# The last 64 channels of gate and up: one pair of half-height products, or two full ones with zero rows in the weight tiles

## The chip, the cores and the metric

The kernel runs on one core of one Trainium2 chip. The metric is the device time of one execution in microseconds; before the change the median of three runs is 2017.08 us (2015.53 to 2045.22). A core has TensorE (PE; its weight loads are listed as PEld), VectorE (DVE), ScalarE (ACT), GpSimd (POOL) and SyncE (SP). SP, ACT and POOL issue the DMA transfers, each in the order of its own queue. Line numbers (L773) are those of the kernel before.

## The reference, cut to what matters

The program computes a block and the gradients of its inputs. The block has a state-space convolution `s` and a gated feed-forward part on the same normalised input, 2048 positions of 576 channels:

```python
xn = _layernorm(x, axis=-1)
s = _A_ref(xn, ...)                      # long convolution, kernel built from A, B, C, dt
gate = jnp.einsum("bsd,df->bsf", xn, w1) # 576 -> 4608
up = jnp.einsum("bsd,df->bsf", xn, w3)   # 576 -> 4608
h = _silu(gate) * up
out = jnp.einsum("bsf,fd->bsd", h, w2)   # 4608 -> 576
return x + s * _silu(out)
```

`jax.vjp` of it then gives the gradients of twelve inputs. What the change touches is the computation of `gate` and `up`. The 576 channels that they sum over are four chunks of 128 and a remainder of 64.

## The kernel before, in words

The work is laid out in stages: a prologue (layer norm, parameters, the transposed input `xnT`), then the state-space forward pass (`ssm_forward`) and the hidden layer of the feed-forward part (`ffn_hidden`) side by side, then the output of the feed-forward part (`ffn_output`), then the backward pass.

Every instruction is traced with a priority, a due time that `self.at(us)` sets; a planner then orders each engine's instructions at build time, by priority among those that are ready in its own model. `ssm_forward` and `ffn_hidden` both start at due time 0 (L1512, L1513), so their instructions are interleaved on all engines. `ssm_forward` generates the convolution's kernel in 36 chunks (matmuls L496 and L532, the latter with 128x64 weights) and then convolves (matmuls L603, L632 and L635, VectorE work L650 to L659).

`ffn_hidden` (L740) runs over nine blocks `fb` of 512 hidden columns, and in each over 16 tiles of 128 positions, two at a time (`NT = 2`). Per block it loads the weights on SP: four chunks of `w1` and four of `w3` (`wmB_w1`, `wmB_w3`, L757), and the tail tile `wtail`, a tile of 128 partitions whose rows 0 to 63 are the last 64 rows of `w1` (L759) and whose rows 64 to 127 are the last 64 of `w3` (L760). `wp` gives two buffers for each of them. The fifth chunk of `xnT` holds the last 64 channels twice, in partitions 0 to 63 and, by a DMA in the prologue (L177), in 64 to 127.

Per tile of positions there are two PSUM tiles, `pg` for gate and `pu` for up (two buffers each), and ten products: four chunks into `pg`, four into `pu` (L773), and then two products over 64 partitions each, one on the upper and one on the lower half of the array's rows:

```python
nc.tensor.matmul(pg[:], lhsT=xnT[0:rem, nfull, ts], rhs=wt[0:rem, :], start=False, stop=True)
nc.tensor.matmul(pu[:], lhsT=xnT[rem:P, nfull, ts], rhs=wt[rem:P, :], start=False, stop=True)
```

ScalarE then applies Silu to `pg` (L777), VectorE or ScalarE copies `pg` out (L779, L781), ScalarE copies `pu` out (L782), and VectorE multiplies (L783). SP stores `h_t` (L785), and POOL stores `g_t` and `u_t` (L787), which the backward pass reads again.

At the end of this stage `ffn_output` loads `w2` in nine groups on POOL (`w2g`, L813) and the transposed hidden rows `hc` on SP (L817, the transfer itself in a helper, L1265), and multiplies them (L828). Its tiles lie in memory that tiles of `ffn_hidden` used: a load waits until those are released. In partition bytes the hidden loop's pools are, one after the other: `wmB_w1` and `wmB_w3` (16 KB), `wtail` (2 KB), `g_t`, `u_t`, `s_t`, `h_t` (6 KB each).

Of the kernel before, what the change touches and what calls it, by code (L numbers as in the profile page):

```python
# [14 lines left out]
BF16 = mybir.dt.bfloat16  # L15
I32 = mybir.dt.int32
I16 = mybir.dt.int16
P = 128
# [43 lines left out]
class K:  # L62
# [674 lines left out]
        self.H_dram = self.dram.tile([LT, P, F], BF16, name="H_dram")  # L737
        self.GS_dram = self.dram.tile([4, P, LT, D // 4], BF16, name="GS_dram")

    def ffn_hidden(self, wp, gup, ps, T0, TA):  # L740
        nc, cfg = self.nc, self.cfg
        D, DT, L, LT, F, FT = cfg.D, cfg.DT, cfg.L, cfg.LT, cfg.F, cfg.FT
        aps = self.aps
        FB = 512
        NT = 2
        ng = FB // self.FG
        nfull = D // P
        rem = D - nfull * P
        assert F % FB == 0 and rem == 64
        xnT = self.xnT  # L750
        for fb in range(F // FB):
            self.at(T0 + TA * 4 * fb)
            f0 = fb * FB
            wm = {}
            for w in ("B_w1", "B_w3"):
                wm[w] = wp.tile([P, nfull, FB], BF16, name="wm" + w)
                nc.sync.dma_start(out=wm[w][:], in_=aps[w][0:nfull * P, f0:f0 + FB].rearrange("(c p) f -> p c f", p=P))  # L757
            wt = wp.tile([P, FB], BF16, name="wtail")
            nc.sync.dma_start(out=wt[0:rem, :], in_=aps["B_w1"][nfull * P:D, f0:f0 + FB])  # L759
            nc.sync.dma_start(out=wt[rem:P, :], in_=aps["B_w3"][nfull * P:D, f0:f0 + FB])  # L760
            for i0 in range(0, LT, NT):
                self.at(T0 + TA * 4 * fb + TA * 4 * i0 // LT)
                g_t = gup.tile([P, ng, NT, self.FG], BF16, name="g_t")
                u_t = gup.tile([P, ng, NT, self.FG], BF16, name="u_t")
                s_t = gup.tile([P, ng, NT, self.FG], BF16, name="s_t")
                h_t = gup.tile([P, NT, FB], BF16, name="h_t")
                for q in range(NT):
                    ts = slice((i0 + q) * P, (i0 + q + 1) * P)
                    pg = ps.tile([P, FB], FP32, name="pg")
                    pu = ps.tile([P, FB], FP32, name="pu")  # L770
                    for (w, pt) in (("B_w1", pg), ("B_w3", pu)):
                        for c in range(nfull):
                            nc.tensor.matmul(pt[:], lhsT=xnT[:, c, ts], rhs=wm[w][:, c, :], start=(c == 0), stop=False)  # L773
                    nc.tensor.matmul(pg[:], lhsT=xnT[0:rem, nfull, ts], rhs=wt[0:rem, :], start=False, stop=True)
                    nc.tensor.matmul(pu[:], lhsT=xnT[rem:P, nfull, ts], rhs=wt[rem:P, :], start=False, stop=True)  # L775
                    pgv = pg[:].rearrange("p (g f) -> p g f", g=ng)
                    nc.scalar.activation(out=s_t[:, :, q, :], in_=pgv, func=ACT.Silu)  # L777
                    if q % 2 == 0:
                        nc.vector.tensor_copy(out=g_t[:, :, q, :], in_=pgv)  # L779
                    else:  # L780
                        nc.scalar.copy(out=g_t[:, :, q, :], in_=pgv)  # L781
                    nc.scalar.copy(out=u_t[:, :, q, :], in_=pu[:].rearrange("p (g f) -> p g f", g=ng))  # L782
                nc.vector.tensor_tensor(out=h_t[:].rearrange("p t (g f) -> p g t f", g=ng), in0=s_t[:], in1=u_t[:],  # L783
                                        op=ALU.mult)
                nc.sync.dma_start(out=self.H_dram[i0:i0 + NT, :, f0:f0 + FB].rearrange("t p f -> p t f"), in_=h_t[:])  # L785
                for (dst, src) in ((self.G_dram, g_t), (self.U_dram, u_t)):
                    nc.gpsimd.dma_start(out=dst[fb * ng:(fb + 1) * ng, :, i0:i0 + NT, :].rearrange("g p t f -> p g (t f)"),  # L787
                                        in_=src[:].rearrange("p g t f -> p g (t f)"))
# [672 lines left out]
@with_exitstack  # L1461
def kernel(
    ctx: ExitStack,
    tc: tile.TileContext,
    A_u: bass.AP,
    A_A_re: bass.AP,
    A_A_im: bass.AP,
    A_B_re: bass.AP,
    A_B_im: bass.AP,
    A_C_re: bass.AP,  # L1470
    A_C_im: bass.AP,
    A_log_dt: bass.AP,
    A_Dskip: bass.AP,
    B_x: bass.AP,
    B_w1: bass.AP,
    B_w3: bass.AP,
    B_w2: bass.AP,
    grad_out: bass.AP,
    out_0: bass.AP,
    out_1: bass.AP,  # L1480
    out_2: bass.AP,
    out_3: bass.AP,
    out_4: bass.AP,
    out_5: bass.AP,
    out_6: bass.AP,
    out_7: bass.AP,
    out_8: bass.AP,
    out_9: bass.AP,
    out_10: bass.AP,
    out_11: bass.AP,  # L1490
    out_12: bass.AP,
):
    aps = dict(A_u=A_u, A_A_re=A_A_re, A_A_im=A_A_im, A_B_re=A_B_re, A_B_im=A_B_im, A_C_re=A_C_re, A_C_im=A_C_im,
               A_log_dt=A_log_dt, A_Dskip=A_Dskip, B_x=B_x, B_w1=B_w1, B_w3=B_w3, B_w2=B_w2, grad_out=grad_out,
               out_0=out_0, out_1=out_1, out_2=out_2, out_3=out_3, out_4=out_4, out_5=out_5, out_6=out_6,
               out_7=out_7, out_8=out_8, out_9=out_9, out_10=out_10, out_11=out_11, out_12=out_12)
    k = K(tc, aps, {})
    with k.ctx:
        k.setup_consts()
        k.persist = k.ctx.enter_context(tc.tile_pool(name="persist", bufs=1))  # L1500
        k.dram = k.ctx.enter_context(tc.tile_pool(name="scratch_dram", bufs=1, space=bass.MemoryType.DRAM))
        k.ffn_scratch()
        mats = ExitStack()
        matp = mats.enter_context(k.pool(name="mats", bufs=1, side="right"))
        k.parp_ctx = ExitStack()
        k.parp = k.parp_ctx.enter_context(k.pool(name="parp", bufs=1))
        with k.pool(name="xT", bufs=1) as xp, k.pool(name="kg_sel", bufs=1) as selp:
            k.prologue(matp, selp, xp)
            with k.pool(name="f_w", bufs=2) as wp, \
                    k.pool(name="f_gu", bufs=3) as gup, \  # L1510
                    k.pool(name="f_ps", bufs=2, space=bass.MemoryType.PSUM) as fps:
                k.ssm_forward(0, 8, 8)  # L1512
                k.ffn_hidden(wp, gup, fps, 0, 12)  # L1513
        k.parp_ctx.close()
        gctx = ExitStack()
        gop = gctx.enter_context(k.pool(name="go_keep", bufs=1))
        k.go_o = gop.tile([P, k.cfg.LT, k.cfg.D], BF16, name="go_o")
        k.gop = gop
        goT = gop.tile([P, k.cfg.DT, k.cfg.L], BF16, name="goT")
        k.goT, k.goTt = goT[:, 0:k.cfg.D // P], goT[:, k.cfg.D // P]  # L1520
        k.nc.gpsimd.memset(k.goTt[k.cfg.D % P:P, :], 0.0)
        k.ffn_output(480, 10)
        k.backward(700, 36, 90, 15, 18, gctx, mats)
# [30 lines left out]
```

## Time and profile before

| | |
|---|---|
| median of three runs | 2017.08 us (2015.53 to 2045.22) |
| the profiled execution's own time | 2026.19 us |
| its span, first to last instruction | 2024.4 us |
| mean granted TensorE clock | 0.967 |
| first and last product of `ffn_hidden` | 133.2 and 661.8 us |
| products L773 (gate, up; 128x512), recorded | 526 into `pg`, 559 into `pu`, 376 to 634 ns, median 379 |
| products L774 and L775 (64x512) | 144 each, median 387 ns |
| weight loads L773, L774 and L775 | 1152 of 98 ns, 144 of 93 and 144 of 93 (medians) |
| weight transfers L759 and L760 | 9 each, landing after 2.9 to 5.2 us |
| first product of `ffn_output` (L828) | 671.8 us |

How to read it: a line of a timeline gives the start in microseconds from the start of the span, the length, the engine, the line of the kernel, the operation, what it writes and reads, its shape and how many of one kind follow each other; in brackets stands the idle time of the engine ahead of it and what ended that. A shape "64*128 64x512" is a product over 64 partitions with 128 columns of weights and 512 moving columns. The length of a product runs from its start to its result, and products are pipelined: a product of 128x512 lasts about 380 ns, but the next one starts well before it has ended. What a product takes from TensorE's time is therefore read from the distance between starts, not from the length. Some matmul records are missing from the trace.

### The profile page before, as it was taken

The numbers are of one execution on the slowest core, as the hardware profiler recorded it, in microseconds if no ns is written. First come the engines' busy times: TensorE is split into PE (matmuls) and PEld (weight loads), VectorE is DVE, ScalarE is ACT, GpSimd is POOL, SyncE is SP. The second block draws the span as 40 slices with busy tenths as digits, with TensorE's granted clock in tenths as the row PEclk, the third lists the DMA queues.
The fourth block names the chain that finished last, engine by engine and source line by source line (L and its number), as shares of the span: only waits on it lengthen the run. The fifth ranks groups of instructions, "written<-read, shape, count | busy, mean of one in ns | idle before, by whom it ended". The sixth has DMA issues, their size and how long they took to land. (4 is left out here: it accounts for less than half of the span.)

```text
span 2024.4 us, 40373 instructions
## 1 busy us (share of the span) xinstructions
PE 1785.9 (88%) x16465; PEld 1311.4 (65%) x16538; DVE 1392.8 (69%) x2142; ACT 888.7 (44%) x1624; POOL 324.3 (16%) x516
## 2 busy tenths in 40 slices
PE   1789999999999799698989989999899887889977
PEld 0444554445555577577878778887687665667865
DVE  7536565565977255459796596948899844789884
ACT  2867777776554111266464656545444310000000
POOL 5002222221212211101010000111011020231021
PEclk9899999999999899899999999999999998999998
DMA  3588777776655988636565374768999899989995
GB/s 82 193 300 296 250 258 264 263 265 229 221 191 160 281 196 198 186 114 178 167 175 179 116 211 148 197 190 215 223 247 233 192 207 221 218 176 222 234 138 94
DMA packets 624649, 411.25 MB, mean 203 GB/s; under 512 B 427664, under 2 KB 565392, under 8 KB 619856
## 3 DMA queue, kind: packets, MB, share of 16 engines
q1 hardware_dynamic: 565776, 276.34, 56.0%
q0 software_dynamic: 30160, 105.61, 15.5%
q10 hardware_dynamic: 28528, 26.72, 5.0%
q8 instruction: 129, 2.11, 0.4%
q14 instruction: 56, 0.46, 0.1%
HBM read 130.65 MB, written 185.65 MB: 156 GB/s over the span
## 5 line engine op out<-in xcount | busy, mean ns | idle before, releaser
L1417 PEld LDWEIGHTS <-acts 128*128 128x128 bf16 x2304 | 228.4, 100 | 95.6 <-DMA acts<-GG_dram 17.4
L1371 PEld LDWEIGHTS <-xn_bf 128*128 128x128 bf16 x2304 | 224.7, 98 | 34.4 <-issue 8.7
L1036 DVE TENSOR_TENSOR pr_q<-et_ps,pz 128x1024 f32<-128x1024 f32 x144 | 176.1, 1223 | 62.8 <-PE et_ps L1031 54.1
L1322 PE MATMUL ph<-w2T,goT 128*128 128x256 bf16 x1440 | 180.6, 278 | 21.7 <-ACT gh L1325 19.0
L1417 PE MATMUL px<-wT,acts 128*128 128x288 bf16 x1408 | 184.3, 291 | 16.2 <-DMA wT<-in_B_w_dram 16.2
L1039 DVE TENSOR_REDUCE S_all<-pr_q 128x32 f32<-128x1024 f32 x144 | 175.4, 1218 | 3.6
L773 PEld LDWEIGHTS <-xnT 128*128 128x128 bf16 x1152 | 105.3, 98 | 107.7 <-issue 23.4
L1322 PEld LDWEIGHTS <-goT 128*128 128x128 bf16 x1440 | 141.7, 100 | 46.4 <-issue 25.3
L1351 PE MATMUL pgw<-go_o,h_n 128*128 128x288 bf16 x1152 | 155.6, 291 | 10.9 <-ACT gw L1355 8.4
L773 PE MATMUL pg<-wmB_w,xnT 128*128 128x512 bf16 x526 | 158.0, 385 | 5.4 <-ACT g_t L781 2.6
L828 PE MATMUL po<-w2g,hc 128*128 128x288 bf16 x1152 | 147.9, 290 | 13.2 <-DMA w2g<-in_B_w_dram 13.2
L773 PE MATMUL pu<-wmB_w,xnT 128*128 128x512 bf16 x559 | 155.4, 383 | 0.9 <-ACT u_t L782 0.5
L777 ACT ACTIVATE s_t<-pg 128x512 bf16<-128x512 f32 x144 | 86.3, 600 | 148.1 <-PE pu L775 118.0
L828 PEld LDWEIGHTS <-hc 128*128 128x128 bf16 x1152 | 112.7, 99 | 44.8 <-issue 14.6
L1373 ACT CAST gw<-pgw 128x256 bf16<-128x256 f32 x144 | 53.9, 375 | 199.6 <-PE pgw L1371 192.1
L1351 PEld LDWEIGHTS <-h_n 128*128 128x128 bf16 x1152 | 113.9, 99 | 40.5 <-issue 8.6
L1371 PE MATMUL pgw<-gu_n,xn_bf 128*128 128x256 bf16 x1152 | 131.5, 272 | 6.0 <-ACT gw L1355 5.9
L1417 PE MATMUL px<-wA,acts 128*128 128x288 bf16 x896 | 120.1, 294 | 17.1 <-DMA acts<-GG_dram 17.1
L787 POOL DMA_DIRECT2D G_dram<-g_t x72 | 52.4, 728 | 498.9 <-ACT g_t L781 480.1
L1371 PE MATMUL pgw<-gg_n,xn_bf 128*128 128x256 bf16 x1152 | 130.0, 273 | 0.0
L497 ACT ACTIVATE cs_k<-et_ps 128x512 bf16<-128x512 int16 x216 | 116.0, 640 | 6.6 <-PE et_ps L496 6.5
L1325 ACT CAST gh<-ph 128x512 bf16<-128x512 f32 x144 | 81.2, 610 | 81.7 <-PE ph L1322 55.1
(285 smaller groups left out, 3329.9 us busy)
## 6 DMA issues: line engine op xcount, KB each, us to landing
G_dram<-g_t POOLq DMA_DIRECT2D x72, 256.0 KB, 3.3
U_dram<-u_t POOLq DMA_DIRECT2D x72, 256.0 KB, 4.3
H_dram<-h_t SPq DMA_DIRECT2D x72, 256.0 KB, 3.1
Q_dram<-q_k SPq DMA_DIRECT2D x36, 512.0 KB, 3.3
h_n<-U_dram POOLq DMA_DIRECT2D x18, 1024.0 KB, 9.2
gg_n<-G_dram POOLq DMA_DIRECT2D x18, 1024.0 KB, 5.7
GU_dram<-gu_n SPq DMA_DIRECT2D x36, 512.0 KB, 4.7
GG_dram<-gg_n SPq DMA_DIRECT2D x36, 512.0 KB, 6.9
```

What stands on the lines that cost most here:

```text
L497: nc.scalar.activation(out=CS[:, :, o:o + 256], in_=pt[:].bitcast(I16)[:, :, 0::2], func=ACT.Sin, scale=6.283184 / 2 ** 16)
L773: nc.tensor.matmul(pt[:], lhsT=xnT[:, c, ts], rhs=wm[w][:, c, :], start=(c == 0), stop=False)
L777: nc.scalar.activation(out=s_t[:, :, q, :], in_=pgv, func=ACT.Silu)
L828: nc.tensor.matmul(po_[:, pi_, 0:pw], lhsT=hc[:, fi, :], rhs=w2[fi][:, po:po + pw], start=(fi == 0), stop=(fi == FT - 1))
L1036: nc.vector.tensor_tensor(out=pr[:].rearrange("p r k e -> p r (k e)"), in0=T[h][:].rearrange("p k z d a -> p (k z d a)")[:, None].to_broad ...
L1039: nc.vector.tensor_reduce(out=self.S_all[:, :, d0:d0 + 4], in_=pr[:].rearrange("p r k (d a) -> p (r k) d a", d=4), op=ALU.add, axis=AX.X)
L1322: self.pe_last = nc.tensor.matmul(ph[j][:, k, :].rearrange("p (a f) -> p a f", f=P), lhsT=lw, rhs=rh, start=(n == 0), stop=(n == nfull))
L1325: self.sc(lambda: nc.scalar.copy(out=gh[:, j], in_=ph[j][:]))
L1351: self.pe_last = nc.tensor.matmul(pgw[pi_][:, 0:pw], lhsT=hn[:, tt, fl * P:(fl + 1) * P], rhs=go_o[:, tt, po:po + pw], start=(tt == 0), st ...
L1371: self.pe_last = nc.tensor.matmul(pw_[:, 0:FG], lhsT=self.xn_bf[:, tt, c * P:(c + 1) * P], rhs=nat[:, tt, :], start=(tt == 0), stop=(tt == ...
L1373: self.sc(lambda: nc.scalar.copy(out=gw[:, c], in_=pw_[:, 0:FG]))
L1417: self.pe_last = nc.tensor.matmul(px[pi_][:, 0:pw], lhsT=act[:, ai, fi, :], rhs=w[:, po:po + pw], start=(n == 0), stop=(n == len(steps) - 1))
```

## The change

Each of the two weight tails gets a tile of its own with all 128 partitions. In the gate's tile, rows 0 to 63 hold the last 64 rows of `w1` and rows 64 to 127 are zero; in the up's tile, rows 0 to 63 are zero and rows 64 to 127 hold the last 64 rows of `w3`. Two such pairs (`wz`, one buffer each, alternating by block) take the place of the two buffers of `wtail`. The zero rows are written once, ahead of the loop, by four memsets on POOL; the loads of each block overwrite only the other rows. The tail products then run over all 128 partitions of the fifth chunk of `xnT`, and the tail of gate stands directly after the four chunks of gate, ahead of those of up. The number of products, weight loads and transfers per tile and block stays the same.

```diff
-    def ffn_hidden(self, wp, gup, ps, T0, TA):
+    def ffn_hidden(self, wp, wz, gup, ps, T0, TA):
...
+        tails = []
+        for i in range(2):
+            tails.append([wz.tile([P, FB], BF16, name=f"wz{i}{k}") for k in range(2)])
+            nc.gpsimd.memset(tails[i][0][rem:P, :], 0.0)
+            nc.gpsimd.memset(tails[i][1][0:rem, :], 0.0)
         for fb in range(F // FB):
...
-            wt = wp.tile([P, FB], BF16, name="wtail")
-            nc.sync.dma_start(out=wt[0:rem, :], in_=aps["B_w1"][nfull * P:D, f0:f0 + FB])
-            nc.sync.dma_start(out=wt[rem:P, :], in_=aps["B_w3"][nfull * P:D, f0:f0 + FB])
+            wt = tails[fb % 2]
+            nc.sync.dma_start(out=wt[0][0:rem, :], in_=aps["B_w1"][nfull * P:D, f0:f0 + FB])
+            nc.sync.dma_start(out=wt[1][rem:P, :], in_=aps["B_w3"][nfull * P:D, f0:f0 + FB])
...
-                    for (w, pt) in (("B_w1", pg), ("B_w3", pu)):
+                    for k, (w, pt) in enumerate((("B_w1", pg), ("B_w3", pu))):
                         for c in range(nfull):
                             nc.tensor.matmul(pt[:], lhsT=xnT[:, c, ts], rhs=wm[w][:, c, :], start=(c == 0), stop=False)
-                    nc.tensor.matmul(pg[:], lhsT=xnT[0:rem, nfull, ts], rhs=wt[0:rem, :], start=False, stop=True)
-                    nc.tensor.matmul(pu[:], lhsT=xnT[rem:P, nfull, ts], rhs=wt[rem:P, :], start=False, stop=True)
+                        nc.tensor.matmul(pt[:], lhsT=xnT[:, nfull, ts], rhs=wt[k][:], start=False, stop=True)
...
-                    k.pool(name="f_gu", bufs=3) as gup, \
+                    k.pool(name="f_wz", bufs=1) as wz, k.pool(name="f_gu", bufs=3) as gup, \
...
-                k.ffn_hidden(wp, gup, fps, 0, 12)
+                k.ffn_hidden(wp, wz, gup, fps, 0, 12)
```

## The prediction

> **What bounds the kernel now.** I read the page first (which engine fills the span), then the table by stages, then TensorE's timeline inside the stage that the change touches, then its waits, then the seam to the next stage.
>
> ```profile
> PE 1785.9 (88%) x16465; PEld 1311.4 (65%) x16538; DVE 1392.8 (69%) x2142; ACT 888.7 (44%) x1624; POOL 324.3 (16%) x516
> ```
>
> The table by stages (columns: the stretch in us, its length, then busy time of each engine). The hidden-layer loop runs from 133 to 662 us, beside the kernel generation of the state-space part up to about 500 us and its convolution after it:
>
> ```profile
> 300.00:350.00 50.00, 48.19 (x535) 24.75 (x541) 28.95 (x41) 35.39 (x72) 10.30 (x15) 1.00 0.76 256
> ...
> 500.00:550.00 50.00, 48.11 (x342) 26.89 (x346) 48.86 (x60) 25.98 (x58) 9.70 (x14) 1.00 0.70 229
> ```
>
> The reader is to see TensorE at 48 of 50 us in both, ScalarE at 35 and then 26, the clock at 1.00. VectorE reaches 49 of 50 once the convolution starts, so from 500 us on it stands beside TensorE as a bound. Up to 500 us TensorE alone sets the pace, and what it saves or pays there moves the end of the stage.
>
> Busy time hides what one product costs in sequence, so I go by start times. TensorE's timeline at 300 us (start, length, engine, line, tiles):
>
> ```profile
> 300.21 1.04 PE L773 MATMUL pg<-wmB_w,xnT 128*128 128x512 bf16 x4
> 301.09 1.03 PE L773 MATMUL pu<-wmB_w,xnT 128*128 128x512 bf16 x4
> 302.05 0.39 PE L774 MATMUL pg<-wtail,xnT 64*128 64x512 bf16 x1
> 302.05 0.39 PE L775 MATMUL pu<-wtail,xnT 64*128 64x512 bf16 x1
> 302.37 0.87 PE L532 MATMUL kps<-v_k,q_k 128*64 128x16 bf16 x44
> ```
>
> The two half-height products L774 and L775 do start together (3 ns apart): they share the array. But they pay for it on both sides. A full product follows the one before it after 0.216 us (four of them last 1.03 us, the last 0.379: 0.651 / 3). The last full product starts at 301.74; the pair starts 0.312 us later, not 0.216; and the next instruction starts 0.32 us after the pair. So entering costs 0.096 us and leaving 0.103 us beyond a product's slot of 0.216, and the first full product after it takes some 0.011 us more (1.04 against 1.03). One pair costs 0.096 + 0.003 + 0.319 + 0.011 = 0.429 us of TensorE, and two full products in a row cost 0.432.
>
> **The change part by part.**
>
> *The pair becomes two full products, 144 times.* By what stands around the pair I count three cases over the stage's timeline.
> - 85 pairs stand between full-height, full-width products: 0.432 - 0.429 = +0.003 us each, +0.3 us.
> - 42 pairs are followed by the 128x64 products of L532, as at 302.37. These are another shape, and a full product pays to switch to them too:
>
> ```profile
> 297.60 0.38 PE L496 MATMUL et_ps<-SEL,lhs_t 128*128 128x256 bf16 x2
> 297.91 0.20 PE L532 MATMUL kps<-v_k,q_k 128*64 128x16 bf16 x1
> ```
>
>   The second L496 starts at 297.71, its slot is 0.109, and L532 starts at 297.91: 0.093 us for the switch. Before: 0.096 + 0.003 + 0.317 = 0.416. After: 0.432 + 0.093 = 0.525. So +0.109 us each, +4.6 us.
> - 17 pairs were torn apart by the planner, so each half runs alone, with both switches:
>
> ```profile
> 308.64 0.39 PE L774 MATMUL pg<-wtail,xnT 64*128 64x512 bf16 x1
> 308.95 0.28 PE L496 MATMUL et_ps<-SEL,lhs_t 128*128 128x256 bf16 x1
> 309.17 0.39 PE L775 MATMUL pu<-wtail,xnT 64*128 64x512 bf16 x1
> 309.49 0.39 PE L496 MATMUL et_ps<-SEL,lhs_t 128*128 128x256 bf16 x2
> ```
>
>   One half costs 0.096 + 0.319, then 0.106 to enter again, 0.319, and 0.011: 0.851 us without the L496 between. Two full products cost 0.432 wherever they stand: -0.419 each, -7.1 us.
>
> Sum: 0.3 + 4.6 - 7.1 = **-2.2 us**.
>
> The Trainium skill, "TensorEngine Tiling (Array Packing)", section Theoretical Speedup, gives up to 2x for a contraction of 64 rows or less, and so speaks against this change: by it the pair would be one slot, and two full products would add 144 x 0.216 = 31 us. The same page says under Key Properties that changing the tiling mode drains TensorE; it names no price, and the 0.096 and 0.103 us above agree with it.
>
> *The order in an iteration.* The tail of gate now stands right after its four chunks, so pg is complete four products (0.86 us) earlier, and ScalarE's Silu on it need not wait for pu. Today ScalarE waits for the end of the pair, 118 us in 109 waits, but it has that time to spare; what counts is TensorE's waiting for free PSUM:
>
> ```profile
> ACT s_t L777 <- PE pu L775: 118.0, 109, 2.8
> ...
> PE pg L773 <- ACT g_t L781: 2.6, 1, 2.6
> ```
>
> With 1.9 us of L773 behind VectorE's g_t and 0.5 behind ScalarE's u_t that is 5.0 us; the gain lies between 0 and 5.0. The 2.6 is one wait at 655 us, where ScalarE was itself held by a DMA, and stays. I take **-1 us**.
>
> *Four memsets of 64x512 on POOL, and two more buffers.* The nearest row, L471's memset of 128x768, takes 0.73 us, so four cost at most 2.9 us of POOL. POOL has nothing to do from its last memset at 37.8 us until its first store at 141.47 (an idle of 103.72 us), and the tiles' space is free by the time the main weights are loaded (125 us). The first pair starts at 136.95. Cost 0; without that cover, at most 2.9 us once, ahead of the first tail product; in POOL's queue only stores stand behind it, none before 141 us. Weight loads keep their number, size and place on SP (x9 at L759 and L760): 0. Each buffer is reused after two blocks, as before: 0.
>
> *The seam at 662 us.* The new tiles take 4 KB a partition where the old took 2, so g_t, u_t, s_t and h_t move up by 2 KB. The first hc tile of the output stage, which today lies above them, then overlaps the last 2 KB of h_t: its load, on SP, waits until the next to last H_dram store has landed. Now the hidden loop's last pair starts at 661.8, SP issues the last H_dram store at 667.84, and then:
>
> ```profile
> 671.80 5.36 PE L828 MATMUL po<-w2g,hc 128*128 128x288 bf16 x28 [9.62 <-DMA w2g<-in_B_w_dram]
> ...
> 680.71 0.75 POOL L813 DMA_DIRECT2D w2g<-in_B_w_dram  x1 [7.32 <-DMA H_dram<-h_t]
> ...
> 689.84 2.56 PE L828 MATMUL po<-w2g,hc 128*128 128x288 bf16 x10 [3.07 <-DMA w2g<-in_B_w_dram]
> ```
>
> TensorE's first row tile there ends at 692.4 whatever hc does, because the last w2 group lands at 689.8. An hc that comes by 683 (72 products are 8.8 us at 0.122, from 160 in 19.46 us between 720 and 740) costs nothing. Stored at 660 to 668 and landed 3 us later, then loaded in 7.1 to 10.7 (the landing times of hc), it comes between 670 and 682. Queued on SP behind the four dskip_row loads and the others there (668.85 to 682), it comes at 692: 692 + 8.8 = 701, +8.5 us. For a gain: with one hc load fewer ahead of the last H_dram stores, those land earlier and the last w2 group with them, at most the 3.07 us that TensorE waits for it. Ends -3 and +8.5; I take **0**, the row at 671.80, which waits for w2 and not for hc.
>
> *The planner's order.* It places instructions by priority and readiness, and readiness shifts. 175 times in the stage it enters a run of L532, about 0.2 us for entry and exit. A fifth more or fewer runs is 35 x 0.2 = 7 us either way. I take 0.
>
> Total -2.2 - 1 = -3.2 us. The profiled execution took 2026.19 us (span 2024.4 and 1.8 around it), 9.1 above the median of the runs, 2017.08; the sum is taken from the median: **2013.9 us**, 2014.
>
> **The rivals.**
> - *The gaps are not from the half-height shape* (slower). If the 0.096 and 0.103 us come from something that stays, the two new products cost a slot each on top: +144 x 0.216 = 31 us, 2048. For it: nothing but that a page of averages can't exclude it. Against it: L773 to L773 shows no such gap, and L496 to L532 shows one just where the shape changes. It decides if the tail products of after start more than 0.3 us after the product before them.
> - *The seam turns into a wait for hc* (+8.5 - 3.2): 2022. For it: the overlap. Against: w2 is late in any case.
> - *The overlap of the loop and the convolution is lost* (slower by over 2%). If the planner puts the hidden loop earlier, the convolution stands alone at the end. Between 500 and 662 us there are 42 iterations of the loop, 42 x 2.16 = 91 us of TensorE, and 71 us are the convolution's. VectorE is busy 138 us there, some 113 of it with the convolution. All 91 us moved ahead give 91 + 113 - 162 = 42 us, 2056, and more if VectorE waits in between. It costs from the point where more than 91 - (113 - 71) = 49 us move ahead of 500 us. Against: the priorities are unchanged.
> - *All bounds of gain together* (-2.2 - 5 - 3 - 7): 2000.
>
> **How the numbers follow.** Forecast 0.73, seam 0.10, gaps stay 0.07, overlap lost 0.05, clearly faster 0.05. Forecast with the bounds: low 2017.1 - 2.2 - 5 - 3 - 7 = 2000; high 2017.1 - 2.2 + 8.5 + 7 = 2030, rounded up to 2031, which holds the seam too. Left out are the two slower rivals and half of the faster one, about 0.15. The other half of that, and runs that scatter (the three shown span 2015.5 to 2045.2), make faster by over 2% 0.04; slower by over 2% is the lost overlap and some of the 2048 case, 0.08; within 2%, about what a measurement of this kernel can tell from no change, 0.88.
>
> **What would show it.** In the changed profile: tail products of 128x512 that start 0.216 us after their neighbour; no 64x512 products; as many L532 runs as now, give or take 35; Silu's wait for pu gone; the first L828 product near 672 and the hidden loop's last near 660. It is wrong if the loop ends more than 10 us away from 662, or if a new wait stands at the seam.

## The result, and the profile after

The changed kernel takes 2047.68 us (median of 20 runs, 2021.37 to 2073.19), the kernel before 2017.19 us (20 runs, 2003.09 to 2060.6). The ratio is 1.0132, with a 95% interval of 1.0105 to 1.0159: 27 us slower, 21 to 32, where 3 us less were forecast and the range ended at 2031. The ratios leave out the runs of a slower state, over 1.5% above the fastest, so that 27 us stand where the medians differ by some 30; the profiled executions of the changed kernel (span 2050.7 us) and of x2_pad below are such slower runs, so the order of work and stage lengths are read from them, and differences of whole kernels from the ratios.

The timeline of TensorE of the changed kernel at 300 us answers to the one shown before the change. L778 are the eight chunks, L779 the two tails, L532 the 128x64 products of the kernel generation.

```profile
300.42 0.20 PE L532 MATMUL kps<-v_k,q_k 128*64 128x16 bf16 x1
300.55 0.39 PE L778 MATMUL pg<-wmB_w,xnT 128*128 128x512 bf16 x1
300.87 0.20 PE L532 MATMUL kps<-v_k,q_k 128*64 128x16 bf16 x1
301.00 0.39 PE L778 MATMUL pg<-wmB_w,xnT 128*128 128x512 bf16 x1
301.32 0.20 PE L532 MATMUL kps<-v_k,q_k 128*64 128x16 bf16 x1
301.45 0.39 PE L779 MATMUL pg<-wz,xnT 128*128 128x512 bf16 x1
301.67 1.03 PE L778 MATMUL pu<-wmB_w,xnT 128*128 128x512 bf16 x4
302.54 0.38 PE L779 MATMUL pu<-wz,xnT 128*128 128x512 bf16 x1
302.75 1.03 PE L778 MATMUL pg<-wmB_w,xnT 128*128 128x512 bf16 x4
```

The lower four lines are what was forecast: a tail starts 0.22 us after the product ahead of it (301.67 + 0.65 = 302.32, then 302.54) and is followed after 0.21, with no gap on either side. The upper lines are not: between single products of the hidden loop stand single products of L532, 16 columns each, and each costs a switch in and a switch out, so that 300.42 to 301.45 holds two products of 0.22 us and three of 16 columns and takes 1.03. The table of waits (130 to 735 us) shows how often. Its first number is the time that TensorE's weight loads idled ahead of L532, the second how many times. Before, and after:

```profile
PEld L532 <- issue: 49.1, 197, 0.4
```

```profile
PEld L532 <- issue: 68.3, 265, 0.4
```

The seam between the hidden loop and the output stage, in the timeline of the changed kernel (L779 is the loop's last product, L789 the store of h_t, L817 the load of w2, L1269 the load of hc, L832 the output stage's first product):

```profile
667.09 0.38 PE L779 MATMUL pu<-wz,xnT 128*128 128x512 bf16 x1
...
669.80 0.39 SPq L789 DMA_DIRECT2D H_dram<-h_t  x1
...
671.08 3.73 POOL L817 DMA_DIRECT2D w2g<-in_B_w_dram  x5
...
672.96 31.49 SPq L1269 DMA_TRANSPOSE hc<-H_dram  x3
...
697.32 12.88 PE L832 MATMUL po<-w2g,hc 128*128 128x288 bf16 x83 [29.85 <-DMA hc<-H_dram]
```

TensorE now stands still from 667 to 697 us, and what ends the wait is hc, not w2. Before, three loads of hc had been issued by 666 us, beside the loop:

```profile
643.91 5.53 SPq L1265 DMA_TRANSPOSE hc<-H_dram  x1
...
650.21 16.36 SPq L1265 DMA_TRANSPOSE hc<-H_dram  x2
```

Now the first of them is issued at 672.96, and the next two stand behind it on SP.

### The profile page after: what moved, and what is told of

Its sections match the earlier page's. It is cut to its first block, busy times and chain, and to the rows that moved or that the text cites. A ratio compares the mean times of both kernels' runs of the same rounds, so it can differ in the third digit from the quotient of the medians.

```text
span 2050.7 us, 40366 instructions
## 1 busy us (share of the span) xinstructions
PE 1797.3 (88%) x16465; PEld 1332.0 (65%) x16538; DVE 1393.5 (68%) x2142; ACT 903.7 (44%) x1624; POOL 326.8 (16%) x520
## 5 line engine op out<-in xcount | busy, mean ns | idle before, releaser
L778 PEld LDWEIGHTS <-xnT 128*128 128x128 bf16 x1152 | 111.1, 97 | 110.7 <-issue 6.2
L832 PE MATMUL po<-w2g,hc 128*128 128x288 bf16 x1152 | 146.5, 289 | 29.9 <-DMA hc<-H_dram 29.9
L778 PE MATMUL pg<-wmB_w,xnT 128*128 128x512 bf16 x517 | 158.9, 382 | 6.4 <-DVE g_t L783 5.2
L1355 PE MATMUL pgw<-go_o,h_n 128*128 128x288 bf16 x1152 | 153.1, 288 | 10.7 <-ACT gw L1359 8.6
L778 PE MATMUL pu<-wmB_w,xnT 128*128 128x512 bf16 x571 | 154.1, 379 | 0.9 <-ACT u_t L786 0.5
L832 PEld LDWEIGHTS <-hc 128*128 128x128 bf16 x1152 | 112.6, 99 | 60.4 <-DMA hc<-H_dram 30.3
```

The lines of the kernel that those rows point to most:

```text
L832: nc.tensor.matmul(po_[:, pi_, 0:pw], lhsT=hc[:, fi, :], rhs=w2[fi][:, po:po + pw], start=(fi == 0), stop=(fi == FT - 1))
L1355: self.pe_last = nc.tensor.matmul(pgw[pi_][:, 0:pw], lhsT=hn[:, tt, fl * P:(fl + 1) * P], rhs=go_o[:, tt, po:po + pw], start=(tt == 0), st ...
```

## The experiments

The change does three things at once: the shape of the tails, the order within an iteration, and the place of the hidden loop's tiles in memory. Four kernels take them apart, four more test what came of that. In each table of lengths, "loop" is from the first to the last product of the hidden loop, "seam" from there to the first product of the output stage, both from TensorE's timeline.

**x2_pad: the place in memory alone.**

```diff
+                    k.pool(name="f_pad", bufs=1) as padp, k.pool(name="f_gu", bufs=3) as gup, \
...
+                pad = padp.tile([P, 1024], BF16, name="pad")
+                k.nc.gpsimd.memset(pad[0:64, 0:512], 0.0)
```

> The kernel before, with half-height pairs and its own order, and 2 KB of unused memory a partition ahead of g_t, so that the hidden loop's tiles lie where the change puts them. The seam theory (the wait for hc is most of the loss): the hidden loop lasts 528 to 529 us as before, the first product of the output stage comes 30 us after the loop's last one instead of 10, the output stage ends some 16 us later (after against before: 856.1 - 834.9 = 21.2, of which 667.1 - 661.8 = 5.3 arose in the loop), and the whole is slower by 16 us, 8 to 24. The rival that the products themselves cost the loss: no difference beyond 3 us.

**x3_late: the shape alone.** The second pair of weight tiles comes from a pool on the right side of memory (`side="right"`), and:

```diff
                         for c in range(nfull):
                             nc.tensor.matmul(pt[:], lhsT=xnT[:, c, ts], rhs=wm[w][:, c, :], start=(c == 0), stop=False)
-                        nc.tensor.matmul(pt[:], lhsT=xnT[:, nfull, ts], rhs=wt[k][:], start=False, stop=True)
+                    for k, pt in enumerate((pg, pu)):
+                        nc.tensor.matmul(pt[:], lhsT=xnT[:, nfull, ts], rhs=wt[k][:], start=False, stop=True)
```

> The full products with zero rows, but both tails behind the eight chunks as before, and the second pair of weight tiles on the other side of memory, so that g_t and what follows lie as before. The price list of the prediction: the switches to the half-height shape go (37 us fewer), the pairs no longer share a slot (some 25 us more), 42 exits to the 128x64 products cost as on record: 2 us less than before, -12 to +2. The rival that the gaps around a pair were not from its shape: 27 to 31 us more.

**x4_early: the order alone.** The kernel before, with each half-height tail moved into the loop over gate and up:

```diff
+                    for (w, pt, r) in (("B_w1", pg, slice(0, rem)), ("B_w3", pu, slice(rem, P))):
...
+                        nc.tensor.matmul(pt[:], lhsT=xnT[r, nfull, ts], rhs=wt[r, :], start=False, stop=True)
```

> The half-height products as before, but the tail of gate directly behind its own four chunks, as in the change; memory as before. In the planner's order the 128x64 products of L532 then stand in 276 runs instead of 187, and the two halves hardly ever stand together. Theory: 90 runs more at 0.19 us are 17 us, and some 125 pairs torn at 0.42 us are 52: 69 us more, 50 to 80. The rival that the order of an iteration costs nothing and a torn pair nothing beyond its missing overlap: 125 x 0.216 = 27 us.

**x1_addr: shape and order, without the place.**

```diff
+                    k.pool(name="f_wz", bufs=1) as wz0, k.pool(name="f_wy", bufs=1, side="right") as wz1, \
...
+            tails.append([wz[i].tile([P, FB], BF16, name=f"wz{i}{k}") for k in range(2)])
```

> The change, with the second pair of weight tiles on the other side of memory, so that g_t and what follows lie as before and hc no longer overlaps h_t. Theory: the hidden loop is as long as in the changed kernel (534 us, 5 more than before), the first product of the output stage follows it after 10 us; the whole is 5 us over before, 0 to 10, so 16 to 22 below the changed kernel. The rival that the loss lies in the products or in the order alone: 20 us or more over before, as the changed kernel.

Measured, with the ratio to the kernel before, run beside each (lengths and runs of L532 from one profiled execution of each):

| | shape | order | place | ratio, 95% interval | loop us | seam us | runs of L532 |
|---|---|---|---|---|---|---|---|
| before | half | tails last | old | 1 | 528.6 | 10.0 | 187 |
| x2_pad | half | tails last | new | 1.0040 [1.0004, 1.0077] | 524.7 | 30.7 | 187 |
| x3_late | full | tails last | old | 0.9945 [0.9907, 0.9984] | 517.2 | 10.8 | 187 |
| x4_early | half | gate first | old | 1.0234 [1.0163, 1.0304] | 591.8 | 11.2 | 276 |
| x1_addr | full | gate first | old | 1.0073 [1.0039, 1.0106] | 539.0 | 11.5 | 276 |
| the change | full | gate first | new | 1.0132 [1.0105, 1.0159] | 534.3 | 30.2 | 276 |

(Before has the order of x2_pad and the change that of x1_addr, whose timelines show 187 and 276 runs; the traces of before and of the change, in which some records are missing, show 175 and 265. For some microseconds of the loop the granted clock was 0.5: 18 us in x4_early, 7 in before, 3.4 or less in the others. That lengthens the loop by at most half as much, 9 us in x4_early.)

Each of the three has its own sign. The shape alone gains 11 us (3 to 19), against the rival of 27 to 31 us more. The place alone costs 8 us (1 to 16), at the low end of what was expected. The seam is 20 us longer in it, and the output stage ends 188 us after the loop instead of 173, 15 us that lie within the interval. The order alone, with half-height tails, costs 47 us (33 to 61) on the whole, where 50 to 80 were expected, and 63 to 67 in the loop of the traced execution, of which up to 9 are its clock; it tears the pairs apart, 285 separate visits to the half-height shape instead of 160. With full products the order costs 0.0128 between x1_addr and x3_late, 26 us, and in the loop 21.8. Over the expected 0 to 10 us, x1_addr is 15 above before (8 to 21): the 5 us that I had read from one trace as the loop's loss were low. The three parts add up to 23 us (-11 for the shape, 26 for the order beside it, 8 for the place), within the change's 21 to 32.

The 21.8 us of loop between x3_late and x1_addr, from the distances between starts in TensorE's timeline less what products of the same form keep (0.216 us for 512 columns): switches into and out of L532 take 39.1 us in x3_late and 57.6 in x1_addr, 18.5 us for 89 runs more, 0.21 us a run, and most of the 21.8.

If the runs are the price, then grouping them must gain in every version, and must make the order indifferent. In `kgen_sum` each of a chunk's 16 pieces has its own due time, half a microsecond after the last. One due time, 20 us earlier, lets the planner put all 64 products of a chunk in one run:

```diff
         for dl in range(DC):
-            self.at(T + TK * dl / DC)
+            self.at(T - 20)
```

**x8_full_r36**: x3_late with this. 

> The full products with tails behind the eight chunks and memory as before (x3_late), and the pieces of a chunk's sum in the kernel generation (L532) get one due time, 20 us ahead of their old one, so that the planner leaves them together: 36 runs of L532 instead of 187. Theory, that a run costs its entry and exit (0.21 us): 151 x 0.21 = 32 us less than x3_late's 0.9945 of before, 0.979 of before, the loop 485 us long. The rival that runs fall where TensorE would wait anyway: within 5 us of x3_late, 0.994.

**x9_early_r36**: x1_addr with this. 

> x1_addr (full products, the tail of gate behind its own chunks, memory as before) with the same one due time, 36 runs of L532 instead of 276. Theory, that the order within an iteration costs only through these runs: as x8_full_r36 within 5 us, 0.979 of before, where x1_addr was 26 us above x3_late. The rival that the early end of gate costs by itself (ScalarE, PSUM): 20 us above x8_full_r36.

**x10_half_r36**: the kernel before with this. 

> The kernel before, with half-height pairs, and the same one due time: 36 runs of L532 instead of 187. Theory: 32 us less than before (0.984). Against x8_full_r36 it shows what the full products are worth where no pair stands before a run of L532: some 10 us (x8_full_r36 the faster). The rival that they are worth nothing: equal.

| | shape | order | ratio, 95% interval | loop us | runs of L532 |
|---|---|---|---|---|---|
| x8_full_r36 | full | tails last | 0.9818 [0.9764, 0.9871] | 495.0 | 36 |
| x9_early_r36 | full | gate first | 0.9822 [0.9764, 0.9879] | 494.8 | 36 |
| x10_half_r36 | half | tails last | 0.9878 [0.9834, 0.9923] | 502.8 | 36 |

x8_full_r36's timeline of TensorE has each chunk in one piece:

```profile
301.61 0.38 PE L778 MATMUL pg<-wmB_w,xnT 128*128 128x512 bf16 x1
302.25 1.19 PE L532 MATMUL kps<-v_k,q_k 128*64 128x16 bf16 x64 [0.26 <-DVE v_k L518]
303.37 0.61 PE L496 MATMUL et_ps<-SEL,lhs_t 128*128 128x256 bf16 x4
```

All three fall, though not by the 32 us expected: x8_full_r36's loop is 495.0 us long and not 485. From x1_addr to x9_early_r36 the loop loses 44.2 us for 240 runs fewer, 0.18 us a run; from x3_late to x8_full_r36 22.2 us for 151, 0.15, less than 0.21, since some of the time goes into waits as in the second line. The edit also moves the pieces 20 us earlier, which could have gained by itself. The switches speak against it: read as above they take 15.9 us in x8_full_r36 and 16.1 in x9_early_r36, 23.2 and 41.5 us less than without the grouping, so they account for nearly all that the loops lost. With the runs gone the two orders are equal (494.8 and 495.0 us): the early end of gate costs nothing by itself in the loop, and gains nothing. (The seam of x9_early_r36 is 19.8 us, that of x8_full_r36 12.2, with memory as before in both; in x9_early_r36 the first product waits for w2, whose loads land after 18.0 us in the median. Why, the runs do not show.) And full products are worth 7.8 us of loop over the half-height pair, of which up to 1.1 are the clock in x10_half_r36; the ratios, 0.9818 and 0.9878, say 12 us, but their intervals overlap, so this rests on one trace of each. Both versions with full products beat both kernels of the case, by 1.8% against before.

**x11_w2_late: why hc is so late at the seam.** In `ffn_output` of x2_pad the first load of hc is traced ahead of the loads of w2, and these move from POOL to SP, behind it:

```diff
+            hc0 = hp.tile([P, FT, P], BF16, name="hc")
+            first = self.nat_transpose(hc0[:], self.H_dram[0])
...
-                nc.gpsimd.dma_start(out=w2g[:], in_=...)
+                with self.tc.issue_after(first.ins):
+                    nc.sync.dma_start(out=w2g[:], in_=...)
```

> x2_pad (the kernel before and 2 KB of unused memory ahead of g_t), with the nine loads of w2 on SP, queued behind the first load of hc, instead of on POOL. In x2_pad that load of hc takes 21 us beside them. If sharing the DMA engines with w2 is what makes hc late: hc lands in 7 to 10 us, the first product of the output stage starts at about 680 instead of 688, and the output stage ends some 5 us sooner than in x2_pad. If the wait for h_t's store alone is: no product sooner than 686, and w2 comes later still, so 5 us slower than x2_pad.

The loads of hc in x2_pad (min, median and longest issue in ns, first and last start; below, the time to landing in us):

```profile
L1265 SPq DMA_TRANSPOSE hc<-H_dram x16: 4412/4958/21225, 663.5 to 816.4; - x16
...
DMA to landing us min/median/max: 7.2/7.4/24.3
```

and in x11_w2_late, where the landing of the first load is not recorded, SP's first loads and TensorE's first product:

```profile
663.41 6.69 SPq L1269 DMA_TRANSPOSE hc<-H_dram  x1
670.20 10.04 SPq L816 DMA_DIRECT2D w2g<-in_B_w_dram  x9
...
675.52 7.66 PE L832 MATMUL po<-w2g,hc 128*128 128x288 bf16 x40 [17.97 <-DMA w2g<-in_B_w_dram]
```

Issued at the same time (663.5 and 663.4), the first load takes 24.3 us to land beside the loads of w2. With w2 behind it, it has landed by 675.5, after 12.1 us at most, since the first product reads it and waits for w2 last. The first product starts at 675.5 instead of 687.9, and the output stage ends at 841.1 instead of 845.4. So both parts are there: the wait until h_t has been stored (663.4 instead of the 643.9 of before), and a load that takes at least 12 us more beside those of w2. The whole is no better (1.0069 [1.0037, 1.0100] against 1.0040). The short seam, 10 to 12 us, stands in the kernels of the first table without the overlap in memory, x1_addr among them, so that is what has to go.

## Why the prediction was wrong

**The price of the pair: right.** One pair costs as much as two full products, and the 0.096 and 0.103 us around it go with its shape: in the changed kernel a tail starts 0.216 us after the full product ahead of it (median of 210). Where next to no pair stands ahead of a run of L532 (x8_full_r36 against x10_half_r36) the loop gains 7.8 us; for that case the list's terms give 7.1 - 0.3 = 6.8. The term of 42 exits to L532 came too: in x3_late all 42 stand there, and L532 starts 0.309 us after a tail in the median, 0.093 more than its slot, as here:

```profile
296.91 0.38 PE L780 MATMUL pu<-wz,xnT 128*128 128x512 bf16 x1
297.22 0.87 PE L532 MATMUL kps<-v_k,q_k 128*64 128x16 bf16 x44
```

Yet x3_late gained 11 us (3 to 19) where the sum had 2.2 of gain, and its loop is 7.5 us shorter than that of x2_pad, a kernel with the same runs of L532. What the list left out is a wait: in x2_pad L532 waits 23 times, 4.0 us in all, for ScalarE's copy of an earlier result out of PSUM (`KT`, L535), in x3_late not at all. The price was right, the gain of the whole too small.

**The planner's order: the step that failed first.** It read "A fifth more or fewer runs is 35 x 0.2 = 7 us either way. I take 0." The 0.2 us were right (0.15 to 0.21 measured), the number of runs was not: 89 more, where 35 were allowed, 18.5 us of switches and 21.8 us of loop. The fifth stood on no row. What should have warned: the change moved a tail by four products within each of 144 iterations, in a stage whose order is not written out but planned, and in which the trace showed 57 of 175 runs to be of one product. Why the planner's order turns out so, the runs do not show; that it does, by the order alone and not by the shape, they do (187 runs with the tails last and 276 with gate first, for either shape).

**The order in an iteration**: a gain of 1 us was taken, none was found (x9_early_r36 against x8_full_r36).

**The seam: the step that failed second.** "I take 0, the row at 671.80, which waits for w2 and not for hc." The overlap had been found, and its price bounded by +8.5; x2_pad puts it at 8 us (1 to 16). What the choice of 0 had wrong is the time at which hc comes: it was to be 670 to 682, with a landing of 7.1 to 10.7 us. The 10.7 is that of the load issued at 660.3, where the first w2 load starts 5 us later; the load at the seam has all nine of w2 beside it and lands after 24.3. The bound is right in part by luck: it had hc at 692 because SP's queue would hold it until 682, and hc came at 697.3, 5.3 us of which are the longer loop, issued at 673.0 already but slow to land. The loads of hc go in order, so the second and third are late with the first, but TensorE waits only for the first (once, 30.3 us in x2_pad). The row that was taken as nearest shows the stage as it is ordered now, and the change alters that order.

**The memsets: right.** They take 0.52 us each at 68 us, in POOL's idle time.

**The rivals.** The measured median of 2047.7 us is the very time that the rival "the gaps are not from the half-height shape" gives, 2048. It is refuted all the same: tails start 0.22 us after their neighbour, and x3_late is faster than before. The time alone would have confirmed a cause that isn't there. The seam's wait for hc did come, but as the smaller part of the loss (8 us beside the 26 of the planner's order), and no case of the forecast held the two together. The loss of the overlap of loop and convolution did not come: the convolution's last product of L632 starts 5.5 us ahead of the loop's last one.

## What to carry to other kernels

Two half-height products that share the array saved nothing here where full products stand on both sides (0.429 us against 0.432), and they lost when the planner tore them apart: count what is paid to enter and to leave a shape, not only the overlap. In a stage that a planner interleaves, the number of changes of shape is a cost of its own; count it in the order of the program before and after an edit, even an edit that moves one instruction, and group small products of another shape on purpose. When a tile grows, look at which later load comes to overlap a tile that is released late, and at what stands behind that load in its queue.

## What the runs showed of the hardware

To enter and leave a run of L532 costs about as much whatever its length: in x1_addr 0.103 and 0.120 us (medians) for the 160 runs of a single product of 128x16, 0.093 and 0.099 for the 24 runs of 40 or more. 64 such products in a row take 1.19 us in x8_full_r36. A transposing load of hc, which lands after 7.1 us at best, takes 24.3 us when the nine w2 loads run beside it.
